# Splitting the float16 halves of key and query chunks in two pieces, in a fused agent-attention and mixture-of-experts kernel

## The chip, the cores and the metric

The kernel runs on one core of one Trainium2 chip. The metric is the device time of one execution in microseconds. TensorE (PE) multiplies matrices, VectorE (DVE) and ScalarE (ACT) do elementwise work, GpSimd (POOL) some more of it, and SyncE (SP) issues nearly all DMAs, in one queue and in order. Each engine works through its own list of instructions in order, and waits on semaphores for the others.

## The reference

There are four batches (B) of 11456 tokens (N) with 128 channels, 49 agents, eight experts with 1024 hidden units. All is float32.

```python
scale = 1.0 / np.sqrt(q.shape[-1])
def sm(a, b):
    s = scale * (a @ b.transpose(0, 2, 1))
    s = s - s.max(-1, keepdims=True)
    e = np.exp(s)
    return e / (e.sum(-1, keepdims=True) + 1e-09)
a2k = sm(agents, k)          # agents look at the keys
agent_v = a2k @ v
q2a = sm(q, agents)          # queries look at the agents
x = (q2a @ agent_v)          # then flattened to B*N tokens
...
expert_idx = np.argmax(x @ w_gate, axis=1)
gate_w = softmax(x @ w_gate)[expert_idx]      # written out in the original
h = np.maximum(xe @ w1[e], 0.0)
out[mask] = gate_w[mask, None] * (h @ w2[e])  # for the tokens of each expert
```

## The kernel before, in words

Tokens of a batch are cut into twelve chunks: eleven of 1024 tokens (a tile of 128 partitions by 8 by 128) and one of 192 (96 partitions by 2 by 128). For each batch the kernel first reads the keys (k) chunk by chunk, then the values (v), then the queries (q), and then sends all tokens of the batch through the one expert that most of them want; tokens of other experts are redone in blocks at the end.

The expert work is what everything else is woven around. It is cut into steps, 184 for a batch (23 groups of up to 512 tokens by 8 slices of the hidden layer), 736 in all. A step is: two matmuls of the first layer into a PSUM tile `ph` (L1535, L1536; four buffers), the ReLU of it on ACT into the high float16 half `hh[:, 0]` (L1538), the low half `hh[:, 1]` on DVE (L1539), and, five steps later, twelve matmuls of the second layer (L1553). Every eighth step DVE scales and empties the output tile (`yo`, L1566). While the steps of batch b run, the keys and values of batch b+1 and the last queries of batch b are prepared between them.

The order of that other work is written out by hand. Every piece of work is an event with a time counted in steps; `at(t, f)` puts it into a heap, `after(dt, f)` puts it dt steps behind the event that runs now. Events are traced in order of their times. Instructions of an event at time t may not stand ahead of the paced step's matmul at t - 1.5 on PE, of its ReLU at t - 2 on ACT, and of its low half at t - 2 on DVE. SP's instructions all stand in the order of their events.

A key or query chunk that is taken in the common way ("A") goes through these events; the lines are those of the profile:

- `use` and `load`: the chunk's load, issued from SP (L350) with up to three uses ahead, into one of eleven `ld` buffers;
- `squares` at t: ACT squares the tile and sums it by partition (L407, tile `jk`);
- `total` at t + 0.5: DVE makes a power-of-two scale of the sum in two tiny instructions, `hb` (L253) and `mul` (L257); POOL makes its inverse `div` (L260);
- `split` at t + 0.8 (batch 0: t + 1): ACT writes the high half of the scaled tile (`hi`, one instruction, L445), and DVE writes the low half (`lo`, one instruction, L449), which needs the high half; both are 128x1024;
- `turn_over` 4.5 steps later (batch 0: 2.5): SP issues a DMA transpose of both halves (L485) into `hT`, which has two buffers for keys and two for queries;
- `kscores` or `qscores` at t + 12 or so: 24 matmuls of `hT` with the agents (L550 to L552), whose results ACT (L579, keys) or DVE (L824, L828, queries) takes on.

Keys and queries of 1024 tokens that are split in this way from the first step on are 70 in number: queries 4 to 10 of batch 0, keys 3 to 10 and queries 0 to 10 of batch 1, keys and queries 0 to 10 of batches 2 and 3. Values go through the same `split` lines, but are not touched by the change. Two chunks (`PRE`: query 3 of batch 0 and key 2 of batch 1) are split before the first step.

Of the kernel before, what the change touches and what calls it, by code (L numbers as in the profile page):

```python
# [16 lines left out]
AF = mybir.ActivationFunctionType  # L17
ALU = mybir.AluOpType
# [32 lines left out]
QA, QB, QC, QB3, KL, LL, UD, RG, D1, DL = -27, 11, 13, 10.5, 12, 9.5, 2, 0.7, 0.5, 0  # L51
# [3 lines left out]
UDL = 1.5  # L55
LHH, LATER = 11, (1, 4, 6)
ES, SV0 = 2, 1.7
TFL = 104.2
VD3, UD0, QD9 = 1.3, 1.2, 1.5
TM2 = 1.7  # L60
QM0, QG0 = (-145.5, -141.85, -137.3), ("K", "V", "V")
KP = 2, 5
LO0, LQ3 = -135.5, -142.9
# [2 lines left out]
PRE = {(0, "q", 3): (-157, -147.5), (1, "k", 2): (-156.9, -145.4)}  # L66
TLQ = 5, 9.5, 14
GL = -141.6, -140.6
KS1 = [-140.6, -139.7] + [0.5 + 8.2 * i for i in range(10)]
KS2 = {0: 1.5, 1: 6.5}  # L70
# [6 lines left out]
DTR, DTQ, DTE, DEX, DST, DXS = 4.5, 2.5, 3, 6, 5, 0.5  # L77
# [18 lines left out]
def agent_moe_kernel(ctx, tc, q, k, v, agents, wg, w1, w2, out):  # L96
    nc = tc.nc
# [8 lines left out]
    chunks = [(c * CH, P, 8) for c in range(NCH)]  # L106
    if REM:
        chunks.append((NCH * CH, REM // 2, 2))
    NCK = len(chunks)
# [7 lines left out]
    scale = 1.0 / math.sqrt(D)  # L117
# [177 lines left out]
    def pick(x, c):  # L295
        return x[c % len(x)]
# [4 lines left out]
    now, count = [0], [0]  # L301

    def at(t, f, *a):
        count[0] += 1
        heapq.heappush(events, (t, count[0], f, a))

    def after(dt, f, *a):
        at(now[0] + dt, f, *a)

    def turns(gen, t, dt, n):  # L310
        for i in range(n):
            at(t + i * dt, next, gen, None)
# [3 lines left out]
    def attention(b):  # L316
        st = state[b]
        base = b * steps
        first, last = b == 0, b + 1 == B

        how = {}
# [110 lines left out]
        def split(src, c):  # L432
            with queued("D") if b < 2 else nullcontext():
                split1(src, c)

        def split1(src, c):
            _, p, t = chunks[c]
            x = loaded[b, src, c]
            hl = xpool.tile([P, 2, 8, D], F16, tag="hl", name="hl", bufs=HLB)
            hi, lo = hl[:, 0], hl[:, 1]  # L440
            m = SC[src, c][0][:p, :1]
            if pick(HI[b > 0][src], c) == "D" or (b, src, c) == (0, "q", 3):
                gate["HQ"] = nc.vector.tensor_scalar(hi[:p, :t, :], x[:p, :t, :], m, None, op0=ALU.mult)
            else:
                nc.scalar.activation(hi[:p, :t, :], x[:p, :t, :], AF.Copy, scale=m)  # L445
            if (b, src, c) in PRE:
                at(1.5 if b else LQ3, split_low, "WL" if b else "V", src, c, x, hl)
            elif pick(LO[b > 0][src], c) == "D":
                nc.vector.scalar_tensor_tensor(lo[:p, :t, :], x[:p, :t, :], m, hi[:p, :t, :], op0=ALU.mult, op1=ALU.subtract)  # L449
                split3(src, c, hl)  # L450
            else:
                after(0 if first else DXS, split2, src, c, x, hl)

        def split_low(behind, src, c, x, hl):
            _, p, t = chunks[c]
            with queued(behind):
                nc.vector.scalar_tensor_tensor(hl[:p, 1, :t, :], x[:p, :t, :], SC[src, c][0][:p, :1], hl[:p, 0, :t, :],
                                               op0=ALU.mult, op1=ALU.subtract)
            split3(src, c, hl)

        def split2(src, c, x, hl):
            _, p, t = chunks[c]
            m, xv = SC[src, c][0][:p, :1], x[:p, :t, :]
            if pick(XS[b > 0][src], c) == "D":
                nc.vector.tensor_scalar(xv, xv, m, None, op0=ALU.mult)
            else:
                nc.scalar.activation(xv, xv, AF.Copy, scale=m)
            nc.gpsimd.tensor_tensor(hl[:p, 1, :t, :], xv, hl[:p, 0, :t, :], op=ALU.subtract)
            split3(src, c, hl)

        def split3(src, c, hl):
            if src == "v":
                TT[src, c] = hl[:, 0], hl[:, 1]
                return
            if (b, src, c) in PRE:
                at(max(now[0], HT0[src]), turn_over, src, c, hl)
            else:
                after(0 if now[0] < 0 else DTQ if first else DTR, turn_over, src, c, hl)

        def turn_over(src, c, hl):  # L480
            _, p, t = chunks[c]
# [367 lines left out]
        def esplit1(c):  # L849
# [8 lines left out]
            if first and c == 2:  # L858
                at(TM2, eturn, c, m2)
            else:  # L860
# [181 lines left out]
        def use(t, src, c):  # L1042
            o = b, src, c
            uses.append((EARLY[o] if o in EARLY else PRE[o][0] if o in PRE else base + t, b, src, c))

        def prepare(t, src, c):
            if (b, src, c) in PRE:
                t = PRE[b, src, c][1] - base
            at(base + t, squares, src, c)
            at(base + t + (0 if first else D1), total, src, c)  # L1050
            at(base + t + (0.5 if first else UD + UDL if (src, c) == ("v", NCK - 1) else UD + UD0 if b > 1 and (src, c) == ("v", 0) else UD), total2, src, c)
            at(base + t + (UD + 1 + SV0 if (src, c) == ("v", 0) and not first else 1 if first else D1 + 0.3 if src != "v" else UD + UDL + 1 if c + 1 == NCK else UD + 1), transposed if how[src, c] in "CX" else split, src, c)

        ks, kt, kl, vt, vl = (KS0, KT0, KL0, VT0, VL0) if first else (KS, KT, KL, VT, VL)
        dl = 0 if first else DL
# [1 line left out]
        for x, f in ((AG0, agent_squares), (AG1, agent_sums), (AG2, agent_scale), (AG3, agent_split)):  # L1057
            at(base + ka - x, f)
        for c in range(NCK):
            t = KS1[c] - base if b == 1 and c < len(KS1) else ks + kt * c  # L1060
            use(t, "k", c)
            prepare(t, "k", c)
            s = KS2[c] - base if b == 1 and c in KS2 else t + kl
            at(base + s, kscores, c)
            at(base + s + dl, kmax, c)
        if b == 1:
            at(-137.35, kpiece, 0, KP[1], "P1")
        if first:
            at(LO0, load_on, 5)
        tk = t + kl + 2  # L1070
        for i in range(1 if first else 0, 3):
            at(base + tk + i, keymax, i)
        tv = tk + 4
        for c in range(NCK):
            t = tv + vt * c
# [25 lines left out]
        for c in range(NCK):  # L1101
            if first and c < NQ:
                t, ql_ = QS0[c], QL0[c]
            else:
                t = (Q0 + QC * (c - 3) if first and c > 2 else QA + QB * c if c < 3 else
                     QA + 2 * QB + (QB3 if last else QC) * (c - 2))
                ql_ = KLL if last and c > 2 else KL
                if not first and c < 2:
                    t, ql_ = (t - QE, ql_) if c == 0 else (t, ql_ + QL1)
            if 0 < b < B - 1 and c == 9:  # L1110
                ql_ += QD9
            use(-150 + 3 * c if first and 0 < c < NQ else t, "q", c)
            prepare(t, "q", c)
            at(base + t + ql_, qscores, c)
            t0, t3 = t + ql_ + DL, t + ql_ + 3
            if first and c < NQ:
                t0, t3 = -135.9 if c == 2 else QM0[c] + 0.1, (-145, -132.6, -132.5)[c]
            at(base + t0, qexp, c)
            tl = max(t + ql_ + (TL if first and c < NQ else LLL if last and c > 2 else LL), ta + (TLM if first else 4) + c / 2)
            if first and c < NQ:  # L1120
                tl = TLQ[c]
            end = min([x for x in starts if x > c] + [NCK]) - 1
            c0 = max(x for x in starts if x <= c)
            late_ = c0 * 16 + LAG + 8 - 6 * RG - 1 - LMG - LSP * (end - c)
            late_ = min(late_, (LT3 if last else LT) - 6 * RG - 1.5 - LSP * (NCK - 1 - c))
            tl = max(tl, min(tl + LX, late_))
            if c > 2 and tl >= t3 + ES + 6.5:
                t3 += ES
            at(base + t3, esplit, c)
            at(base + tl, logits, c)  # L1130
            if c + 1 in starts or c == NCK - 1:
                turns(route(c), base + tl + 1, RG, 6)
                tf = max(tl + 1 + 6 * RG, tw + 1)
                at(base + tf, factors, c)
                c0 = max(x for x in starts if x <= c)
                assert tf < c0 * 16 + LAG + 8, (b, c, tf)
# [477 lines left out]
    for b in range(B):  # L1614
        attention(b)
        steps_of.append(experts(b))
        turns(steps_of[b], b * steps, 1, steps + LAG + 2)
        turns(leftover_ranks(b), b * steps + (LT3 if b + 1 == B else LT), LTS3 if b + 1 == B else LTS, 6)

    for j in range(2 * E):  # L1620
        b, i = divmod(j, -(-2 * E // (B - 1)))
# [105 lines left out]
```

## Time and profile before

| | us |
|---|---|
| median of 3 runs (1076.25 to 1080.18) | 1076.61 |
| the profiled execution's own time | 1071.08 |
| its span, first to last instruction | 1069.3 |
| PE busy in the span | 1006.5 |
| DVE busy | 977.8 |
| ACT busy | 828.2 |

The profiled execution is one of its own, some 5 us quicker than the shown runs. The span is what the trace covers; 1.8 us of the execution lie around it. Busy times are those of the engine's instructions; a wait inside the program is the idle time ahead of an instruction, together with what ended it.

### The profile page before, as it was taken

Reading aid. Unit: us, or ns where it says so; the run is one execution under the profiler, and the core shown is the slowest. Engines: PE = TensorE matmul, PEld = TensorE weight load, DVE = VectorE, ACT = ScalarE, POOL = GpSimd, SP = SyncE. Lnnn points to the kernel's source line nnn. Section 1 sums busy time; section 2 is a strip of 40 time slices with the busy share of each in tenths; the row PEclk is TensorE's granted clock in tenths of the full one; section 3 lists DMA queues with packets and bytes.
Section 4 is the critical chain, followed back from the end, with each engine's and each line's share of the span. In section 5 each row is a group of like instructions: output and inputs, shape, how many; then the busy total and the mean of one; then the engine's idle time right before and its main releaser. Section 6 shows DMA issues by size and latency. Waiting matters only on the chain.

```text
span 1069.3 us, 35681 instructions
## 1 busy us (share of the span) xinstructions
PE 1006.5 (94%) x14586; PEld 816.8 (76%) x14586; DVE 977.8 (91%) x2256; ACT 828.2 (77%) x1519; POOL 251.5 (24%) x457
## 2 busy tenths in 40 slices
PE   7989999999999999999999999999999999999986
PEld 7878778777777877777777877777778778767885
DVE  5789999999999998999999998999999999899893
ACT  6668887888788878988788877988677667667674
POOL 1100001236100101334200001333200235171283
PEclk9999999999999999999999999999999999999999
DMA  9889998534699997544699997544556664434550
GB/s 322 273 228 216 203 215 188 140 96 150 166 233 227 222 190 198 159 148 163 160 242 220 225 190 201 154 160 144 144 132 145 159 142 102 148 116 147 170 194 16
DMA packets 265368, 188.39 MB, mean 176 GB/s; under 512 B 207129, under 2 KB 231282, under 8 KB 265200
## 3 DMA queue, kind: packets, MB, share of 16 engines
q1 hardware_dynamic: 263632, 183.82, 67.2%
q0 software_dynamic: 1568, 2.25, 1.1%
q8 instruction: 115, 1.88, 0.7%
q14 instruction: 53, 0.43, 0.1%
HBM read 99.75 MB, written 36.43 MB: 127 GB/s over the span
## 4 chain that ended last, share of the span: by engine, by line
DVE 43%; PE 28%; ACT 12%; issue 9%; DMA 3%; POOL 3%; SPq 0%; POOLq 0%; DVEq 0%; ACTq 0%
DVE hh L1539 16%; PE py L1553 13%; DVE hl L449 8%; PE ph L1535 5%; PE ph L1536 4%; ACT hh L1538 3%; ACT hl L445 3%; DVE yo L1566 3%; ACT jk L407 2%; DVE S L640 1%; DVE mq L824 1%; DVE mx L603 1%; DMA ld<-in_q_dram 1%; DVE E L828 1%; POOL out_dram L1437 1%
## 5 line engine op out<-in xcount | busy, mean ns | idle before, releaser
L1553 PEld LDWEIGHTS <-hh 128*128 128x128 f16 x8640 | 543.5, 98 | 165.5 <-issue 2.0
L1553 PE MATMUL py<-w2h,hh 128*128 128x128 f16 (+1 forms) x5760 | 601.8, 219 | 1.4 <-DVE Ld L878 0.9
L1553 PE MATMUL py<-w2l,hh 128*128 128x128 f16 (+1 forms) x2880 | 520.2, 219 | 0.0
L1539 DVE SCALAR_TENSOR_TENSOR hh<-ph,hh 128x512 f16<-128x512 f32 (+1 forms) x736 | 478.2, 668 | 21.8 <-ACT hh L1538 19.6
L1538 ACT ACTIVATE hh<-ph 128x512 f16<-128x512 f32 (+1 forms) x736 | 410.0, 581 | 96.5 <-PE ph L1536 90.2
L1535 PE MATMUL ph<-M,Ah 128*128 128x512 f16 (+1 forms) x736 | 274.0, 372 | 21.0 <-DVE hh L1539 20.4
L1536 PE MATMUL ph<-M,Al 128*128 128x512 f16 (+1 forms) x736 | 274.1, 373 | 0.0
L449 DVE SCALAR_TENSOR_TENSOR hl<-ld,mul,hl 128x1024 f16<-128x1024 f32 (+1 forms) x113 | 138.9, 1230 | 14.8 <-ACT hl L445 14.2
L445 ACT ACTIVATE hl<-ld,mul 128x1024 f16<-128x1024 f32 (+1 forms) x114 | 124.3, 1091 | 34.9 <-DVE mul L257 34.3
L407 ACT ACTIVATE jk<-ld 128x1024 f16<-128x1024 f32 (+1 forms) x122 | 122.2, 1001 | 6.1 <-DMA ld<-in_k_dram 4.1
L260 POOL TENSOR_SCALAR div<-hb,bits 128x1 int32<-128x1 int32 (+1 forms) x86 | 25.4, 295 | 378.6 <-DVE hb L253 372.7
L1536 PEld LDWEIGHTS <-Al 128*128 128x128 f16 x736 | 71.7, 97 | 28.9 <-issue 27.2
L1535 PEld LDWEIGHTS <-Ah 128*128 128x128 f16 x736 | 73.4, 100 | 2.0 <-issue 1.4
L1566 DVE TENSOR_TENSOR yo<-py,cs 128x512 f32<-128x512 f32 (+1 forms) x92 | 61.6, 670 | 0.9 <-PE py L1553 0.9
L657 POOL TENSOR_TENSOR es<-es,S 128x392 f32<-128x392 f32 (+1 forms) x33 | 32.2, 976 | 110.1 <-ACT S L645 99.1
L550 PE MATMUL ps_s<-agh,hT 128*128 128x49 f16 x572 | 51.8, 184 | 1.8 <-DMA hT<-hl 1.8
L551 PE MATMUL ps_s<-agl,hT 128*128 128x49 f16 x572 | 51.6, 184 | 0.0
L552 PE MATMUL ps_s<-agh,hT 128*128 128x49 f16 x572 | 51.6, 184 | 0.0
L550 PEld LDWEIGHTS <-hT 128*128 128x128 f16 (+1 forms) x590 | 47.9, 97 | 4.3 <-issue 2.1
L551 PEld LDWEIGHTS <-hT 128*128 128x128 f16 (+1 forms) x590 | 46.7, 96 | 0.6
L552 PEld LDWEIGHTS <-hT 128*128 128x128 f16 (+1 forms) x590 | 46.4, 96 | 0.0
L645 ACT ACTIVATE S<-S,ln 128x392 f32<-128x392 f32 (+1 forms) x48 | 27.6, 597 | 21.9 <-DVE S L640 21.7
(328 smaller groups left out, 1385.7 us busy)
## 6 DMA issues: line engine op xcount, KB each, us to landing
ld<-in_k_dram SPq DMA_DIRECT2D x44, 512.0 KB
ld<-in_v_dram SPq DMA_DIRECT2D x44, 512.0 KB
ld<-in_q_dram SPq DMA_DIRECT2D x44, 512.0 KB
out_dram<-yo SPq DMA_DIRECT2D x88, 256.0 KB
w2e<-in_moe_w_dram SPq DMA_DIRECT2D x18, 512.0 KB
w1e<-in_moe_w_dram SPq DMA_DIRECT2D x17, 512.0 KB
exps<-E SPq DMA_DIRECT2D x44, 196.0 KB
wn<-in_moe_w_dram SPq DMA_DIRECT2D x16, 512.0 KB
```

What stands on the lines that cost most here:

```text
L407: nc.scalar.activation(jk[:p, :t * D], x[:p, :t, :].rearrange("p t d -> p (t d)"), AF.Square, accum_out=ss[:p])
L445: nc.scalar.activation(hi[:p, :t, :], x[:p, :t, :], AF.Copy, scale=m)
L449: nc.vector.scalar_tensor_tensor(lo[:p, :t, :], x[:p, :t, :], m, hi[:p, :t, :], op0=ALU.mult, op1=ALU.subtract)
L550: nc.tensor.matmul(o, x[:, 0, i, :p], AG["h"], start=True, stop=False)
L551: nc.tensor.matmul(o, x[:, 0, i, :p], AG["l"], start=False, stop=False)
L552: nc.tensor.matmul(o, x[:, 1, i, :p], AG["h"], start=False, stop=True)
L1535: x1 = nc.tensor.matmul(ph[:, :nn], st['Ah'][:, f, :], m, start=True, stop=False)
L1536: nc.tensor.matmul(ph[:, :nn], st['Al'][:, f, :], m, start=False, stop=True)
L1538: x2 = nc.scalar.activation(hh[:, 0, :nn], ph[:, :nn], AF.Relu)
L1539: x3 = nc.vector.scalar_tensor_tensor(hh[:, 1, :nn], ph[:, :nn], 0.0, hh[:, 0, :nn], op0=ALU.max, op1=ALU.subtract)
L1553: mm_ = lambda l, r, **k: nc.tensor.matmul(o, l, r, skip_group_check=True, **k)
L1566: nc.vector.tensor_tensor(yo[:p, :n, :], py[:p, :n * D].rearrange("p (i d) -> p i d", d=D), cs.unsqueeze(2).broadcast_to([p, n, D]), op=AL ...
```

## The change

A key or query chunk of 1024 tokens that is split after time 0 is split in two pieces of 128x512 (four of the eight token slots each): `piece(0)` at the split's time, `piece(4)` two steps later (`HPC`), each with its own ACT and DVE instruction. The split's event comes one step later after the squares (`SPL`); `turn_over` follows the second piece by 2.5 steps (batch 0: 1.5) so that, counted from the squares, it comes one step later than before (batch 0: two). For the keys of batches 2 and 3 and for queries 0 to 8 (in batch 0: 5 to 8) the load, the squares, the scale and so the whole row come a step sooner (`KE`), and the scores stay where they were.

So for those chunks the squares move a step ahead, the first piece and the transpose stay at their old times, and the second piece comes two steps behind the first. For keys 3 to 10 of batch 1 and queries 9 and 10 the squares stay, the first piece comes one step later, the second three steps later, the transpose one step later (batch 0, queries 4, 9 and 10: two). Chunks of 192 tokens stay in one piece, a step later after their squares.

```diff
@@ -439,6 +442,15 @@  (split1)
             m = SC[src, c][0][:p, :1]
+            if now[0] > 0 and t == 8 and src != "v":
+                def piece(i):
+                    nc.scalar.activation(hi[:, i:i + 4], x[:, i:i + 4], AF.Copy, scale=m)
+                    nc.vector.scalar_tensor_tensor(lo[:, i:i + 4], x[:, i:i + 4], m, hi[:, i:i + 4], op0=ALU.mult, op1=ALU.subtract)
+                    if i:
+                        split3(src, c, hl)
+                piece(0)
+                after(HPC, piece, 4)
+                return
             if pick(HI[b > 0][src], c) == "D" or (b, src, c) == (0, "q", 3):
@@ -475,7 +487,7 @@  (split3)
-                after(0 if now[0] < 0 else DTQ if first else DTR, turn_over, src, c, hl)
+                after(0 if now[0] < 0 else DTQ - (SPL if (b, src, c) not in PRE else 0) if first else DTR - SPL - (HPL if chunks[c][2] == 8 else 0), turn_over, src, c, hl)
@@ -1049,7 +1061,7 @@  (prepare)
-            at(... 1 if first else D1 + 0.3 if src != "v" else ..., transposed if how[src, c] in "CX" else split, src, c)
+            at(... 1 + (SPL if base + t > 2 else 0) if first else D1 + 0.3 + SPL if src != "v" else ..., transposed if how[src, c] in "CX" else split, src, c)
@@ -1057,17 +1069,17 @@  (keys of a batch)
-            t = KS1[c] - base if b == 1 and c < len(KS1) else ks + kt * c
+            t = KS1[c] - base if b == 1 and c < len(KS1) else ks + kt * c - (KE if b > 1 else 0)
-            s = KS2[c] - base if b == 1 and c in KS2 else t + kl
+            s = KS2[c] - base if b == 1 and c in KS2 else t + kl + (KE if b > 1 else 0)
-        tk = t + kl + 2
+        tk = t + kl + 2 + (KE if b > 1 else 0)
@@ -1109,6 +1121,8 @@  (queries of a batch)
+            if not (first and c < 5) and c < 9:
+                t, ql_ = t - KE, ql_ + KE
```

with `SPL = 1`, `KE = 1`, `HPC, HPL = 2, 1`; before, `D1` is 0.5, `DTQ` 2.5 and `DTR` 4.5.

## Rows read from the trace of the kernel before

**Rows 1.** Windows: stretch, length; busy us of PE, PEld, DVE, ACT, POOL; clock.
```profile
67.00:184.00 117.00, 113.20 (x1685) 90.28 (x1684) 111.51 (x241) 94.56 (x168) 8.32 (x21) 1.00 0.97 219
...
264.00:424.00 160.00, 153.22 (x2287) 122.40 (x2285) 151.17 (x361) 129.19 (x230) 16.99 (x39) 1.00 0.89 205
...
508.00:664.00 156.00, 149.01 (x2216) 119.14 (x2214) 147.57 (x356) 127.06 (x228) 17.41 (x46) 1.00 0.95 210
...
750.00:910.00 160.00, 155.37 (x2161) 123.48 (x2161) 151.37 (x384) 113.60 (x215) 37.86 (x76) 1.00 0.60 138
```

**Rows 2.** Page, part 4: the chain that ended last, by engine.
```profile
DVE 43%; PE 28%; ACT 12%; issue 9%; DMA 3%; POOL 3%; SPq 0%; POOLq 0%; DVEq 0%; ACTq 0%
```

**Rows 3.** Waits of PE in the four stretches in order (total us, times, longest).
```profile
PE ph L1535 <- DVE hh L1539: 1.6, 4, 0.8
...
PE ph L1535 <- DVE hh L1539: 3.4, 6, 1.0
...
PE ph L1535 <- DVE hh L1539: 3.1, 6, 1.0
...
PE ph L1535 <- DVE hh L1539: 3.5, 8, 1.3
```

**Rows 4.** Waits of DVE for the high half, first and last of the four stretches.
```profile
DVE hl L449 <- ACT hl L445: 2.0, 4, 0.6
...
DVE hl L449 <- ACT hl L445: 1.0, 3, 0.6
```

**Rows 5.** Waits of ACT, whole span.
```profile
ACT hl L445 <- DVE mul L257: 34.3, 48, 1.9
```

**Rows 6.** Timeline of ACT, 389 to 395 us (start, us, line, what).
```profile
389.07 1.05 ACT L407 ACTIVATE jk<-ld 128x1024 f16<-128x1024 f32 x1
...
390.11 1.14 ACT L445 ACTIVATE hl<-ld,mul 128x1024 f16<-128x1024 f32 x1
391.15 1.07 ACT L1538 ACTIVATE hh<-ph 128x512 f16<-128x512 f32 x2
```

**Rows 7.** Timeline of DVE, the same stretch.
```profile
391.28 1.28 DVE L449 SCALAR_TENSOR_TENSOR hl<-ld,mul,hl 128x1024 f16<-128x1024 f32 x1
392.49 1.28 DVE L1539 SCALAR_TENSOR_TENSOR hh<-ph,hh 128x512 f16<-128x512 f32 x2
393.68 1.28 DVE L449 SCALAR_TENSOR_TENSOR hl<-ld,mul,hl 128x1024 f16<-128x1024 f32 x1
```

**Rows 8.** Timeline of PE: two steps without a wait, then the same stretch.
```profile
352.81 0.38 PE L1535 MATMUL ph<-M,Ah 128*128 128x512 f16 x1
...
353.91 0.38 PE L1535 MATMUL ph<-M,Ah 128*128 128x512 f16 x1
...
393.22 0.38 PE L1535 MATMUL ph<-M,Ah 128*128 128x512 f16 x1 [0.89 <-DVE hh L1539]
```

**Rows 9.** Timelines of DVE and ACT, 14 to 18 us: scaled halves of 128x512.
```profile
14.08 1.40 DVE L523 SCALAR_TENSOR_TENSOR xT<-pxT,mul,xT 128x512 f16<-128x512 f32 x2
15.40 0.35 DVE L595 COPY mx<-S 128x392 f32<-128x392 f32 x1
...
15.90 1.27 ACT L522 ACTIVATE xT<-pxT,mul 128x512 f16<-128x512 f32 x2 [0.40 <-DVE mul L257]
```

**Rows 10.** Timelines of DVE, SP, ACT and PE: key 3 of batch 3, a load.
```profile
562.01 1.29 DVE L449 SCALAR_TENSOR_TENSOR hl<-ld,mul,hl 128x1024 f16<-128x1024 f32 x1 [0.20 <-ACT hl L445]
...
557.30 0.42 SPq L350 DMA_DIRECT2D ld<-in_k_dram  x1
...
563.36 2.81 SPq L485 DMA_TRANSPOSE hT<-hl  x1
...
563.81 1.05 ACT L407 ACTIVATE jk<-ld 128x1024 f16<-128x1024 f32 x1
...
569.44 0.20 PE L550 MATMUL ps_s<-agh,hT 128*128 128x49 f16 x1
```

**Rows 11.** Waits of PE, 508 to 664 us: the one wait for a transpose.
```profile
PE ps_s L550 <- DMA hT<-hl: 1.8, 1, 1.8
```

More of the change, by code (lines that the diff above doesn't have):

```diff
@@ L60 @@
 TM2 = 1.7
+SPL = 1
+KE = 1
+HPC, HPL = 2, 1
 QM0, QG0 = (-145.5, -141.85, -137.3), ("K", "V", "V")
@@ L1051, in prepare @@
             at(base + t + (0.5 if first else UD + UDL if (src, c) == ("v", NCK - 1) else UD + UD0 if b > 1 and (src, c) == ("v", 0) else UD), total2, src, c)
-            at(base + t + (UD + 1 + SV0 if (src, c) == ("v", 0) and not first else 1 if first else D1 + 0.3 if src != "v" else UD + UDL + 1 if c + 1 == NCK else UD + 1), transposed if how[src, c] in "CX" else split, src, c)
+            at(base + t + (UD + 1 + SV0 if (src, c) == ("v", 0) and not first else 1 + (SPL if base + t > 2 else 0) if first else D1 + 0.3 + SPL if src != "v" else UD + UDL + 1 if c + 1 == NCK else UD + 1), transposed if how[src, c] in "CX" else split, src, c)
         ks, kt, kl, vt, vl = (KS0, KT0, KL0, VT0, VL0) if first else (KS, KT, KL, VT, VL)
```

## The prediction

> **What bounds the kernel now.** I read the windows view first, over the four stretches in which keys and queries are split and no values are [rows 1]. The reader is to see that two engines are full at once: of 593 us PE is busy for 570.8 and DVE for 561.6, so PE idles for 22.2 us and DVE for 31.4. ACT is busy for 464.4 and idles for 128.6. PE runs at full clock in all of them. Neither PE nor DVE can give much by itself; what can be got are the moments in which one waits for the other. The chain that ended last says the same of the whole span, with DVE ahead of PE and ACT third [rows 2].
>
> The waits say who holds whom. In these stretches PE stood 24 times, 11.6 us, in front of a step's first matmul until DVE had finished a low half and so freed a buffer of `ph` [rows 3]; that is half of PE's idle time there. DVE itself stood 20 times, 9.0 us over the four (from 2.0 in the first to 1.0 in the last), in front of a chunk's low half (L449) until ACT had written its high half (L445) [rows 4]. And ACT stood 48 times in the whole span, 34.3 us, in front of the high half until DVE had made the scale [rows 5].
>
> The timelines show how these hang together at one place. On ACT the squares (389.07) are followed by the high half (390.11) with no ReLU between them, so the step's next ReLU starts at 391.15, 2.08 us after the squares [rows 6]. DVE can start the low half at 391.28 only; the ReLU's low halves behind it start at 392.49 [rows 7]. PE, which needs the first of them, stood 0.89 us, until 393.22 [rows 8]. A step on PE that waits for nothing takes 353.91 - 352.81 = 1.10 us [rows 8], so one such pile-up eats most of what four `ph` buffers can bridge.
>
> **The change part by part.**
>
> *Two instructions for one, on DVE.* 70 chunks get a second low half. Two scaled halves of 128x512 took 15.40 - 14.08 = 1.32 us from start to start, 0.66 each [rows 9]; one of 128x1024 takes 392.49 - 391.28 = 1.21 [rows 7]. Instructions overlap their neighbours' ends, so starts are what counts: 1.32 - 1.21 = 0.11 us a chunk, 70 x 0.11 = 7.7 us more DVE work. Those of rows 9 read PSUM and ours read SBUF; the shape and the per-partition scale are the same, so I take their price. From below: an unscaled ReLU half of 128x512 takes (393.68 - 392.49) / 2 = 0.595 [rows 7], which makes two no dearer than one, 0. From above: by durations, 0.74 (1.40 less 0.66) twice against 1.28, 0.20 a chunk, 14 us. Nothing excludes any of these. Not all of it is paid in time: 7.7 us stand against 31.4 us of DVE's idle time in those stretches, but idle time at the wrong place doesn't help, and the chain runs mostly over DVE. I take +2 us, a quarter; the ends are 0 and the whole 14.
>
> *Two instructions for one, on ACT.* Two high halves of 128x512 took 1.27 us [rows 9], one of 128x1024 1.14 [rows 6]: 70 x 0.13 = 9.1 us. I cost them at nothing: ACT's 128.6 idle us hide them [rows 1]. Without that cover each would delay a ReLU by 0.13 us.
>
> *What the pieces take off the waits.* In the place of one 1.21 us block on DVE there are two of 0.66, two steps apart, so a ReLU's low half behind a piece comes 0.55 us sooner. The first high half takes ACT 1.27 / 2 = 0.64 instead of 1.14, about as long as DVE is busy with the ReLU half ahead of it (0.595), so DVE's wait for it, 9.0 / 20 = 0.45 us each [rows 4], should go. And with the squares a step further ahead, or the split a step later, a ReLU stands between squares and first piece and the scale is ready: ACT's wait for the scale, 34.3 / 48 = 0.71 us each [rows 5], should mostly go for keys and queries. These three are one chain, so I count only its end, PE's waits: 24 of 0.48 us each [rows 3]. A pile-up that loses 0.55 and often 0.45 more loses most such waits; but several of the 24 have no key or query split ahead of them. I take 9 of the 11.6 us. The ends are 0 (the waits move to other places) and 20: the 11.6, and DVE's 9.0 going to stretches where DVE is late without PE being seen to stand for it (11.6 + 9.0, rounded down).
>
> *The transpose.* SP's place for it is unchanged for most chunks, but in the place shown it already starts only 0.06 us after the low half ends (563.36 against 562.01 + 1.29) [rows 10], so it will start as much later as the second piece ends later: two steps, 2.2 us, and 0.66 - 1.21 = -0.55, together some 1.7 us; a step more for keys of batch 1. It was issued by 566.17 and its matmul came at 569.44, 3.27 us later [rows 10]; 1.6 us stay for its landing. In SP's timeline 18 of the 70 stand at most 4.3 us apart in this way. The stretch holds one wait for a transpose, 1.8 us, so landings are not far from mattering even now [rows 11]. What is queued on SP behind it (stores of `yo`, loads, the transpose of `mm`) waits as long. I take +1 us: one or two scores that stand for half a us or so. From below 0, from above 18 x 0.6 = 11 us (18 late by 0.6 each: half of the 1.7, less what has slack).
>
> *The moved loads.* Load and squares move together. A load whose issue ended at 557.72 has its squares at 563.81, 6.1 us later [rows 10]; if SP stands 1.7 us longer, 4.4 are left. I cost it at nothing, since ACT's waits in these stretches hold none for a load; without that slack it would be up to 1.7 us for a chunk. Ten small chunks and key 2 of batch 1 only have their split a step later: nothing.
>
> *A rule of the Trainium skill.* Rows 1 have DVE busy for 561.6 of 593 us, 95%, and ACT for 78%. The Trainium skill, Perfetto Trace Analysis, section Optimizing Scalar/DVE Operations, says that "grouping and performing larger operations can improve throughput if the engine is saturated", with about 60 ns of overhead for a DVE operation on SBUF, and that breaking up instructions may help where Scalar and Vector aren't saturated but cause bubbles elsewhere. For DVE it is the first sentence that applies, and it speaks against the change; for ACT the second. By its figure the added DVE work would be an estimated 4.2 us, and paid in full it would be a slower kernel unless the bubbles are worth more.
>
> *Sum.* -9 + 2 + 1 = -6 us. The profiled execution, 1071.1 us with a span of 1069.3, would come to 1065.1; it was quicker than the three runs shown, so on their median of 1076.6 I expect 1070.6.
>
> **The rivals.**
>
> *The waits only move.* Everything is at its place, but DVE is as full as before, and what PE gains at one step it stands for at a later one. For it: both engines at 95% or more [rows 1]. Against: PE's idle time is in few, short waits [rows 3]. Time: -2 to +2, 1076.
>
> *More falls than the waits counted.* DVE's own waits turn into time as well: -18 + 2 + 1 = -15, 1061.6. For it: DVE leads the chain [rows 2]. Against: PE was busy for 96% of these stretches [rows 1], so there are only 22.2 us to take.
>
> *The transpose comes late: slower.* Place: the first score matmul of a chunk (L550). Price: at 11 us instead of 1 the sum is -9 + 2 + 11 = +4, 1080.6. It decides where landing takes over 1.6 us after the issue ends. For it: the wait of 1.8 us [rows 11]. Against: it is a single one among 70.
>
> *DVE is the bound and the work is paid in full: slower.* This is the mechanism of the rule above, by the rows: at 14 us added, of which all counts, and 5 of the 9 us regained, 14 - 5 + 1 = +10, 1086.6. For it: DVE's 43% of the chain [rows 2]. Against: 31.4 us idle.
>
> **How the numbers follow.** Forecast 0.50, waits only move 0.17, more falls 0.15, transpose late 0.12, DVE paid in full 0.06. Half a per cent, 5.4 us, is about what a measurement of this kernel can tell from no change, so the forecast itself (-6, likely -2 to -11) lies close to that line: 0.28 of its 0.50 falls on the faster side, 0.22 on the same. With all of "more falls", faster is 0.43. Same: 0.22 + 0.15 + 0.02 of the late transpose = 0.39. Slower: the other 0.02, 0.10 and 0.06 = 0.18. The range reaches to 1061 (below it about half of "more falls") and to 1081 (above it half of "transpose late" and all of the last).
>
> **What would show it.** Right: 140 pieces of 128x512 at the lines of the high and the low half; DVE busy some 8 us up, ACT some 9; waits of L449 for L445 in these stretches near 2 us instead of 9; PE's waits for L1539 near 4 instead of 11.6. The prediction is wrong if PE shows new waits at L550 for `hT` of 3 us or more in sum, if the pieces take over 0.70 us from start to start, or if PE's waits for L1539 stay above 8 us.

## The result and the profile after

The changed kernel is slower: median 1087.51 us (1083.93 to 1092.03, six executions) against 1077.18 us of before (1076.25 to 1080.18, six), ratio 1.0093, 95% interval 1.0073 to 1.0112. Measured again it gave 1.0076 (1.0044 to 1.0108), and a third time 1.0049 (1.0023 to 1.0075), so 5 to 10 us are lost where 6 were forecast as gained.

The execution profiled after took 1091.71 us, span 1089.6, which is 20.3 more than the span of before. By PE's first step matmul (L1549 now, L1535 before) the first step starts 5.5 us later (72.53 against 67.07), the steps take 14.7 us more, and the rest 0.1. Some 7 of the 14.7 are not the change's: from step 46 to 138 of batch 3 PE stands in short waits with no releaser. Waits of this kind stand at the same steps in the trace of h1 below (5.9 us), whose batches 1 to 3 are before's. They are in just the six traces (after, e9, f1, g6, h1, h4) beside which before itself measured 1077 to 1079 us instead of 1071 to 1072.

The new names: L1549 and L1550 are the `ph` matmuls, L1553 the ReLU's low half, L447 and L448 the pieces (high, low), L457 and L461 what stays whole, L562 the first score matmul, L888 the logits, L890 their reduction.

Windows of the four stretches after, cut at the steps at which [rows 1] were cut:

```profile
72.50:193.60 121.10, 117.83 (x1710) 93.32 (x1710) 111.62 (x255) 96.06 (x180) 9.38 (x22) 0.96 0.83 192
274.10:436.50 162.40, 154.47 (x2285) 123.42 (x2283) 153.93 (x383) 132.74 (x253) 17.65 (x39) 0.99 0.87 202
520.50:676.60 156.10, 149.62 (x2222) 119.62 (x2222) 150.60 (x376) 130.75 (x248) 17.00 (x45) 1.00 0.90 210
762.00:928.60 166.60, 159.61 (x2173) 125.34 (x2173) 154.53 (x396) 115.58 (x227) 35.91 (x76) 0.99 0.58 135
```

The stretches are longer, and the clock is no longer 1.00 in all of them. Waits of PE in the four in order, each stretch behind "..." (total us, times, longest), beside [rows 3] and [rows 11]:

```profile
PE py L1567 <- DVE Ld L890: 1.9, 1, 1.9
...
PE ph L1549 <- DVE hh L1553: 0.2, 1, 0.2
...
PE ph L1549 <- DVE hh L1553: 2.3, 4, 0.8
PE ps_s L888 <- DMA M<-mm: 1.8, 1, 1.8
...
PE ps_s L562 <- DMA hT<-hl: 1.6, 2, 1.2
PE ph L1549 <- DVE hh L1553: 1.5, 5, 0.3
...
PE ph L1549 <- DVE hh L1553: 2.6, 6, 1.3
```

The waits that the change was counted on did fall, from 11.6 us to 6.6. In their place are single long ones: for the logits' reduction, for `M`, for `hT`. The page's groups of the pieces:

```profile
L447 ACT ACTIVATE hl<-ld,mul 128x512 f16<-128x512 f32 x140 | 97.9, 718 | 14.2 <-DVE mul L260 13.8
L448 DVE SCALAR_TENSOR_TENSOR hl<-ld,mul,hl 128x512 f16<-128x512 f32 x140 | 104.9, 753 | 1.6 <-ACT hl L447 1.2
```

There are 140 pieces. ACT's wait for the scale is 13.8 us instead of 34.3 [rows 5], DVE's for the high half 1.2 over the whole span. DVE is busy 985.1 us, 7.3 more than before; this total is a rough measure, since it is 13.2 us up in e3, which has the same pieces, and 6.3 in e4, which has none.

The prologue, on PE, after:

```profile
58.24 0.31 PE L765 MATMUL ps_small<-ident,av 128*128 128x128 f32 x1
59.92 1.12 PE L971 MATMUL pa<-w1e,av 128*128 128x512 f32 x2 [1.37 <-DMA w1e<-in_moe_w_dram]
60.88 0.71 PE L526 MATMUL pxT<-ident,ld 128*128 128x128 f32 x3
```

and before:

```profile
58.86 0.31 PE L753 MATMUL ps_small<-ident,av 128*128 128x128 f32 x1
59.01 1.04 PE L514 MATMUL pxT<-ident,ld 128*128 128x128 f32 x8
60.78 1.10 PE L959 MATMUL pa<-w1e,av 128*128 128x512 f32 x2 [0.74 <-ACT xF L520]
```

Before, eight transposes `pxT` fill the time until the expert's weights `w1e` have landed. After, `pa` comes first and PE stands 1.37 us for them, instead of 0.74 us for ACT. Windows of after with the granted clock (third number from the end):

```profile
61.00:78.00 17.00, 17.00 (x71) 13.38 (x70) 7.00 (x27) 7.60 (x15) 1.61 (x3) 0.50 0.96 298
132.70:136.10 3.40, 3.40 (x36) 2.40 (x32) 2.89 (x5) 1.19 (x2) 0.91 (x1) 0.50 1.49 217
392.10:395.50 3.40, 3.40 (x26) 2.64 (x24) 2.31 (x7) 1.36 (x3) 0.00 (x0) 0.50 0.92 178
774.40:777.80 3.40, 3.40 (x22) 2.45 (x21) 2.33 (x10) 0.65 (x2) 0.00 (x0) 0.50 0.12 22
```

The clock is at 0.50, 1.2 GHz, for 17 us right behind that stand, and for 3.4 us behind each of three others: for the reduction (PE resumed at 131.75), for `M` (391.57) and for `avs` (773.2). Before, no step ran at half clock.

### The profile page after: what moved, and what is told of

Same layout as the page of the kernel before. It is cut to its first block, busy times and chain, and to the rows that moved or that the text cites. A ratio compares the mean times of both kernels' runs of the same rounds, so it can differ in the third digit from the quotient of the medians.

```text
span 1089.6 us, 35840 instructions
## 1 busy us (share of the span) xinstructions
PE 1020.9 (94%) x14586; PEld 824.9 (76%) x14586; DVE 985.1 (90%) x2326; ACT 840.1 (77%) x1589; POOL 251.8 (23%) x457
## 4 chain that ended last, share of the span: by engine, by line
DVE 37%; PE 34%; ACT 11%; issue 7%; DMA 5%; POOL 4%; SPq 1%; another core or an unknown queue 0%; POOLq 0%; ACTq 0%; DVEq 0%
PE py L1567 15%; DVE hh L1553 15%; PE ph L1549 5%; PE ph L1550 5%; DVE hl L448 4%; ACT hh L1552 3%; ACT jk L410 3%; DVE hl L461 2%; DVE yo L1580 2%; DVE S L652 1%; ACT hl L457 1%; DVE mq L836 1%; DMA ld<-in_q_dram 1%; DMA out_dram<-yo 1%; ACT hl L447 1%
## 5 line engine op out<-in xcount | busy, mean ns | idle before, releaser
L1553 DVE SCALAR_TENSOR_TENSOR hh<-ph,hh 128x512 f16<-128x512 f32 (+1 forms) x736 | 479.0, 665 | 28.2 <-ACT hh L1552 24.9
L1549 PE MATMUL ph<-M,Ah 128*128 128x512 f16 (+1 forms) x736 | 276.5, 376 | 18.8 <-DVE hh L1553 17.5
L1550 PE MATMUL ph<-M,Al 128*128 128x512 f16 (+1 forms) x736 | 276.5, 376 | 0.5 <-issue 0.5
L263 POOL TENSOR_SCALAR div<-hb,bits 128x1 int32<-128x1 int32 (+1 forms) x86 | 28.3, 331 | 370.0 <-DVE hb L256 369.4
L447 ACT ACTIVATE hl<-ld,mul 128x512 f16<-128x512 f32 x140 | 97.9, 718 | 14.2 <-DVE mul L260 13.8
L448 DVE SCALAR_TENSOR_TENSOR hl<-ld,mul,hl 128x512 f16<-128x512 f32 x140 | 104.9, 753 | 1.6 <-ACT hl L447 1.2
L1550 PEld LDWEIGHTS <-Al 128*128 128x128 f16 x736 | 72.2, 98 | 27.8 <-issue 26.7
L1549 PEld LDWEIGHTS <-Ah 128*128 128x128 f16 x736 | 74.0, 101 | 3.1 <-issue 2.5
L562 PE MATMUL ps_s<-agh,hT 128*128 128x49 f16 x572 | 52.1, 184 | 2.5 <-DMA hT<-hl 1.6
L457 ACT ACTIVATE hl<-ld,mul 128x1024 f16<-128x1024 f32 (+1 forms) x44 | 43.7, 1000 | 12.9 <-DVE mul L260 12.6
L461 DVE SCALAR_TENSOR_TENSOR hl<-ld,mul,hl 128x1024 f16<-128x1024 f32 (+1 forms) x43 | 48.9, 1139 | 4.5 <-ACT hl L457 3.7
L562 PEld LDWEIGHTS <-hT 128*128 128x128 f16 (+1 forms) x590 | 48.0, 97 | 3.8 <-DMA hT<-hl 2.0
L563 PEld LDWEIGHTS <-hT 128*128 128x128 f16 (+1 forms) x590 | 46.8, 97 | 1.7 <-issue 1.4
```

What stands on the lines that cost most here:

```text
L447: nc.scalar.activation(hi[:, i:i + 4], x[:, i:i + 4], AF.Copy, scale=m)
L448: nc.vector.scalar_tensor_tensor(lo[:, i:i + 4], x[:, i:i + 4], m, hi[:, i:i + 4], op0=ALU.mult, op1=ALU.subtract)
L562: nc.tensor.matmul(o, x[:, 0, i, :p], AG["h"], start=True, stop=False)
L563: nc.tensor.matmul(o, x[:, 0, i, :p], AG["l"], start=False, stop=False)
L1549: x1 = nc.tensor.matmul(ph[:, :nn], st['Ah'][:, f, :], m, start=True, stop=False)
L1550: nc.tensor.matmul(ph[:, :nn], st['Al'][:, f, :], m, start=False, stop=True)
```

## The experiments

My theory at the start was A with B, with C as the rival; the others came up on the way. **A**: the prologue's new order costs. **B**: late transposes cost (rival of the prediction). **C**: the added DVE work is paid (the other rival); **C0**: only in batch 0. **D**: the later splits cost by themselves. **The waits only move**: even with nothing late there is no gain.

**e1: two keys' transposes back.** Keys 0 and 1 of batch 1 are not split but transposed on TensorE, and the line that moves the splits moves them too.

```diff
-D1 + 0.3 + SPL if src != "v"
+D1 + 0.3 + SPL * (b != 1 or src != "k" or c > 1) if src != "v"
```

> The changed kernel, with one thing undone: the transposes on TensorE of keys 0 and 1 of batch 1, which the diff moved a step later together with the splits, are back in their old place, so that eight of them stand again between the small sum and the product pa in the prologue. Theory A (the prologue: PE reaches pa sooner, stands 1.4 us for w1e, falls to half clock at 61 us and runs 17 us so): the first step starts at 67 us again instead of 72.5, and the time falls by 5.5 to 8 us, to a ratio to before of 1.002 to 1.004. Rival B (the steps alone make the loss, the prologue's delay is taken up by what follows): the time stays at 1.007 to 1.011.

Measured: 1.0041 (1.0025 to 1.0058). The first step starts at 66.83, and the window from 60.6 to 78 has clock 1.00. A holds for this part; about half of the loss is left, measured against the changed kernel's 1.0093 and 1.0076 (against its third measurement, 1.0049, most of it). Waits of PE in the four stretches of e1:

```profile
PE ph L1549 <- DVE hh L1553: 1.4, 3, 0.8
...
PE ps_s L562 <- DMA hT<-hl: 0.6, 1, 0.6
...
PE ph L1549 <- DVE hh L1553: 2.0, 4, 0.8
PE ps_s L888 <- DMA M<-mm: 1.8, 1, 1.8
PE ps_s L562 <- DMA hT<-hl: 1.4, 3, 1.0
...
PE ps_s L562 <- DMA hT<-hl: 2.2, 3, 1.4
PE ps_s L888 <- DMA M<-mm: 1.9, 1, 1.9
...
PE ph L1549 <- DVE hh L1553: 1.0, 3, 0.3
...
PE ph L1549 <- DVE hh L1553: 2.4, 5, 1.2
```

Here the waits for the low half are 6.8 us, 4.8 less than before; those for `hT` and, behind them in SP's queue, for `M` are 7.9 us where before had 1.8. How far such sums move from one execution to another is seen in e2, whose order in these stretches is before's: 9.2 and 2.9. The other four traces with this order (after, e8, e9, f1) have 5.5 to 6.6 and 3.8 to 6.5, so the fall and the rise are there in all five, and the fall goes 2 to 4 us beyond e2's.

**e2: only that, in the kernel before.**

```diff
-D1 + 0.3 if src != "v"
+D1 + 0.3 + ((b, src) == (1, "k") and c < 2) if src != "v"
```

> The kernel before, with one thing done: the transposes on TensorE of keys 0 and 1 of batch 1 a step later, as in the changed kernel; no pieces, no other move. Theory A: PE stands for w1e in the prologue, the clock falls there, the first step starts some 5 us later, and the time rises by 5 to 8 us, ratio 1.005 to 1.0075. Rival B: within 0.2% of before.

Measured: 1.0030 (1.0005 to 1.0055), below A's range, with an interval that reaches into B's. In the profiled execution PE stands 1.34 us for `w1e`, the clock is at half from 60.6 to 64.0, and the first step starts at 68.97, 1.9 us late. The twelve executions lie in two groups: nine from 1070.5 to 1076.0 us at mean clocks of 0.991 to 0.997, three from 1080.0 to 1083.0 at 0.980 to 0.988. A's mechanism is in the trace; its size is open.

**e3: only the cut, in place** (`SPL = 0`, `KE = 0`, `HPC, HPL = 0, 0`).

> The kernel before with the key and query splits in two pieces, one right behind the other in the old place: no step between them, no split or load moved, transposes in their old place. Theory C (the 7.3 us more on DVE are paid in full, as DVE leads the chain): ratio 1.006 to 1.008. Rival B (the loss comes from transposes that start later behind the second piece): the second piece ends only 0.1 us later than the whole did, so within 0.2% of before, at most +2 us.

Measured: 1.0044 (1.0027 to 1.0061), with PE's waits for `hT` and `M` at 1.0 us over the span. So there is a loss with no transpose late. It lies below C's range and above B's; C looked right, at a smaller price.

**e4: whole, but late.** The whole split is put off by `HPC` in place of the pieces; the two keys are back as in e1.

```diff
+if not late and now[0] > 0 and chunks[c][2] == 8 and src != "v":
+    after(HPC, split1, src, c, True)
+    return
```

> The changed kernel with the two keys of e1 back in their old place, and with each key or query split whole again, at the time of the second piece; loads and transposes as in the changed kernel. No DVE work is added. Theory B (late transposes): PE stands for hT at the score matmuls and, behind the queue of transposes, for M at the logits, 4 us or more in sum, and the time is above before by 4 to 8 us, 1.004 to 1.0075. Rival C (the added DVE work): within 0.2% of before or faster.

Measured: 1.0082 (1.0053 to 1.0111). The size is above B's, but the mechanism is B's only in part: PE's waits for transposes add up to 3.0 us over the span, and those for the ReLU's low half rose from before's 20.4 to 24.7. So it doesn't tell a late transpose from a whole block at another place.

**e5, e6, e7: the distance.** All are e1 with, in turn, `HPC, HPL = 0, -1`; the same with whole halves; and `HPC, HPL = 1, 0`.

> As e1 (the changed kernel, keys 0 and 1 of batch 1 transposed in their old place), with the second piece right behind the first instead of two steps later; loads, splits and SP's place for the transposes as in the changed kernel. Theory B (late transposes): the second piece ends two steps, 2.2 us, sooner, PE's waits for transposes fall from e1's 9.6 us to 3 or less, and the ratio from 1.004 to 0.998 to 1.000. Rival C (added DVE work, as e3 showed 1.0044 for it): it stays at 1.003 to 1.005.

> As e5 with the split whole, in one instruction on each engine: only the loads a step sooner and the splits a step later are left of the change, and SP's place for the transposes. Theory C: no DVE work is added, so it is faster than e5 by 3 to 5 us; with the gain that the prediction put on the squares lying further ahead, 0.995 to 0.999. Theory B alone: like e5, within 0.2%. Rival D (the splits a step later cost something by themselves): above 1.002.

> As e1 with the second piece one step after the first instead of two. Theory B: PE's waits for transposes lie between those of e1 (9.6 us) and of e5, about 5, and the ratio is 1.000 to 1.003. Rival C: as e1, 1.004, whatever the distance.

Measured: 1.0041 (1.0023 to 1.0059), 1.0054 (1.0035 to 1.0074), 1.0054 (1.0037 to 1.0072). None is told from e1. In e5 PE waits 0.7 us for transposes in the four stretches instead of e1's 7.9, as B expected, but the time stayed: B falls as the cause of the loss. (The expectations' 9.6 us is more than the 8.0 that e1's trace shows for `hT` and `M` over the whole span.) The waits for the low half went back from 6.8 to 10.8:

```profile
PE ph L1549 <- DVE hh L1553: 1.7, 4, 0.8
...
PE ph L1549 <- DVE hh L1553: 3.6, 5, 1.7
...
PE ph L1549 <- DVE hh L1553: 2.2, 5, 0.5
...
PE ph L1549 <- DVE hh L1553: 3.3, 8, 0.8
```

So the distance between the pieces goes with fewer of those waits and with later transposes: at no step between them, e3 and e5 have 9.8 and 10.8 us of the first, e7 with one step 7.9, the kernels with two 5.5 to 6.8. In time the two about cancel. e6 has no added DVE work and is no faster, which speaks against C as well; it lies in D's range, though its trace has another wait, told at g6.

**e8, e9: the changed kernel again.**

> The changed kernel once more, on the chip of e5 to e7. Theory A: beside e1's 1.0041 it has the prologue's 2 us that e2's trace showed (first step at 69.0 instead of 67.1) or, where the clock stays at half for 17 us, about 8; ratio 1.006 to 1.010. The stalls of batch 3 (6.9 us from its step 46 to 138 in the first profile, with no releaser in the trace) are not in e1, whose order there is the same: if they belong to the kernel they come again, if they were of that one execution they don't.

> The changed kernel once more, on the chip of f1, for the comparison. As in e8 there should be two groups of times, some 4 us above before and some 11 us above it, the upper one at lower clocks; ratio 1.006 to 1.010 by how many fall into which. Theory A1: the upper group is there and f1 has none of it. Rival A2: both kernels have the same groups.

Measured: 1.0076 (1.0044 to 1.0108) and 1.0049 (1.0023 to 1.0075). e8 has two groups, five executions from 1074.3 to 1075.6 at clocks of 0.991 to 0.995 and six from 1082.1 to 1087.7 at 0.981 to 0.992; e9 isn't in two groups and lies below its expected range; it spreads from 1079.6 to 1094.1, its two longest at 0.983 and 0.981. e8's lower group is 3.2 us above its before (1074.67 against 1071.44), no more than e1's 4.4, so what sets e8 apart from e1 is its upper group. The waits without a releaser in batch 3 came again in e9, beside a before of 1078.1 us, and not in e8, beside one of 1071.4: they aren't the kernel's.

The windows behind the stand for `w1e` in e2, e8 and e9 (stands of 1.34, 1.72 and 1.19 us), with the clock third from the end:

```profile
60.60:64.00 3.40, 3.40 (x14) 2.47 (x13) 1.44 (x6) 0.00 (x0) 0.00 (x0) 0.51 0.91 316
...
60.60:67.40 6.80, 6.80 (x31) 5.75 (x29) 1.66 (x7) 1.76 (x3) 0.90 (x1) 0.50 1.11 281
...
61.00:84.80 23.80, 23.80 (x115) 19.25 (x113) 13.00 (x37) 10.36 (x20) 2.02 (x3) 0.50 0.92 234
```

In all four traces in which `pa` stands in this way (these and after) the clock is at half from 60.6 or 61.0 on, for 3.4 to 23.8 us. In the thirteen traces with the two keys' transposes in their old place it is 1.00 from 58 to 66 us. The first step is late by about half of the time at half clock that lies ahead of it: 1.9 us for 3.4, 3.3 (70.39) for 6.8, 5.5 for 11.5 and 6.0 (73.10) for 12.1. So the traces show no delay in the prologue besides the half clock.

**g1: batch 0 as before.** `L` is `(b > 1 or (b == 1 and src == "q"))`; pieces, later splits and their shorter delays hold only where `L`, and queries are loaded sooner only for b > 0.

> The changed kernel with the whole change (pieces, splits a step later, queries' loads a step sooner) kept out of batch 0, whose order is that of before, prologue included; from batch 1 on as changed. Theory C0 (in batch 0 the added DVE work is paid, +2.9 us in e1's trace, and from batch 1 on gain and late transposes nearly cancel): some 3 us less than e1, ratio 1.000 to 1.002. Rival (the loss is spread over all batches): as e1, 1.003 to 1.005.

Measured: 1.0010 (0.9995 to 1.0026). C0's place holds: batch 0 is worth e1's 1.0041 less 1.0010, 3.3 us (the two intervals just touch). Whether it is the added work that is paid there this doesn't tell.

**h1, h4: the two halves of batch 0.** h1 is e3 with pieces only for batch 0's queries and batch 1's keys. h4 has no pieces, `SPL` only for keys of batch 1 from number 2 on, `KE` only for queries 5 to 8 of batch 0.

> As e3 (splits in two pieces, one right behind the other in the old place, nothing moved), but only for the chunks split during batch 0 (its queries and the keys of batch 1); batches 1 to 3 as before. Theory C0 (the added DVE work is paid in batch 0): most of e3's 1.0044, that is 1.0025 to 1.004, with PE at step 45 standing over 2 us for DVE's reduction of the logits instead of 1.1. Rival (the added work is paid wherever pieces are): about a third of e3's, 1.001 to 1.002.

> The complement in batch 0: splits whole, but a step later for the keys of batch 1 from number 2 on, and the last queries of batch 0 loaded a step sooner with their split at the old place, as in the changed kernel; no pieces, and batches 1 to 3 as before. Theory C0 (in batch 0 the pieces cost, not the moves): within 0.15% of before. Rival D (the later split costs): 1.002 or more.

Measured: h1 1.0044 (1.0024 to 1.0063), h4 1.0024 (1.0004 to 1.0044). h1 cuts 15 chunks and costs what e3's 70 cost, so C falls: 15 x 0.12 is only 1.8 us of DVE work, and the other 55 cuts, 6.6 us of it, cost nothing that the two ratios (each good to some 2 us) can tell. h4 lies above C0's expectation and in D's, with an interval that reaches down to 1.0004: the moves cost something in batch 0 as well. What the pieces of h1 do is seen at step 45 on DVE:

```profile
125.10 0.68 DVE L1553 SCALAR_TENSOR_TENSOR hh<-ph,hh 128x512 f16<-128x512 f32 x1
125.70 1.74 DVE L448 SCALAR_TENSOR_TENSOR hl<-ld,mul,hl 128x512 f16<-128x512 f32 x2
127.36 0.29 DVE L890 TENSOR_REDUCE Ld<-ps_y 128x72 f32<-128x144 f32 x1
```

and on PE:

```profile
127.71 0.26 PE L1567 MATMUL py<-w2h,hh 128*128 128x128 f16 x1 [2.37 <-DVE Ld L890]
```

The same place before, on DVE and on PE:

```profile
124.48 0.68 DVE L1539 SCALAR_TENSOR_TENSOR hh<-ph,hh 128x512 f16<-128x512 f32 x1
125.08 0.30 DVE L878 TENSOR_REDUCE Ld<-ps_y 128x72 f32<-128x144 f32 x1
125.78 1.28 DVE L449 SCALAR_TENSOR_TENSOR hl<-ld,mul,hl 128x1024 f16<-128x1024 f32 x1 [0.40 <-ACT hl L445]
```

```profile
125.43 0.22 PE L1553 MATMUL py<-w2h,hh 128*128 128x128 f16 x1 [0.93 <-DVE Ld L878]
```

Before, the low half stands behind the reduction that frees a PSUM buffer for `py`. Cut, its pieces stand ahead of it, and PE waits 2.37 us instead of 0.93. Why they come ahead of it there the traces don't show. In h1 the clock then is at half from 127.6 to 131.0. A second such place follows: the logits (L888) wait 1.8 us instead of 0.7 for `yo`, and the clock is at half from 165.2 to 168.6. e3's trace has both stands (2.4 and 1.8 us) with no half clock behind them, and its first 184 steps take 3.9 us more than before's, so the half clock isn't needed for the loss. In the changed kernel the first is the wait of 1.9 us shown above; the second is 0.9 us there. These stands and the half clock behind them are what the trace shows of the 4.7 us; the rest isn't assigned.

**g2, g6, g7: nothing late.** g2 is g1 with `KE = 3` and `HPC, HPL = 2, -1`; g6 has `KE = 2` and `HPC, HPL = 1, -1`; g7 is g6 with keys 0 to 3 of batches 2 and 3 whole and in their old places.

> As g1, with keys and queries loaded and squared three steps sooner instead of one, so that the first piece comes two steps before the place in g1 and the second ends about when the whole low half ended before; SP's place for the transposes as before. Theory B (from batch 1 on only the late transposes eat the gain): PE's waits for transposes fall to 2 us or less, the shorter waits for the ReLU's low half stay, and it is faster than before by 2 to 5 us, ratio 0.995 to 0.998. Rival (the waits only move): within 0.2% of g1.

> As g2 (batch 0 as before, pieces from batch 1 on, the second on time), with the pieces one step apart and the loads two steps sooner instead of three. If the gain of the pieces is there to be had once nothing comes late: 0.995 to 0.998. If the waits only move, as g2 showed: 0.999 to 1.002.

> As g6, with keys 0 to 3 of batches 2 and 3 (those split around the turn of a batch) whole and at their old places too, so that no squares wait there for a load that stands on SP behind two transposes (g6: 5.6 us on ACT, 4.2 us on PE, half clock for 6.8 us after it). If that was what ate the gain in g6: 0.996 to 0.999. If there is no gain to be had from pieces: 0.999 to 1.002, as g6.

Measured: 1.0016 (0.9997 to 1.0035), 1.0004 (0.9983 to 1.0026), 1.0002 (0.9988 to 1.0017). g6's trace has one late load at the turn of a batch. SP's timeline there, and the waits from 311 to 320 us:

```profile
298.82 9.57 SPq L497 DMA_TRANSPOSE hT<-hl  x2
308.44 0.57 SPq L353 DMA_DIRECT2D ld<-in_k_dram  x1
```

```profile
ACT jk L410 <- DMA ld<-in_k_dram: 5.6, 1, 5.6
...
PE py L1567 <- ACT hh L1552: 4.2, 1, 4.2
```

The key's load stands behind two transposes on SP, the squares that now come sooner wait for it, and the ReLU queued behind them too; e6 has the same at the same place (6.2 us on ACT, 3.8 on PE). g7 takes this out and still ends at before. Its waits for the low half in the four stretches, with none for a transpose, are 13.5 us:

```profile
PE ph L1549 <- DVE hh L1553: 1.6, 4, 0.8
...
PE ph L1549 <- DVE hh L1553: 5.3, 7, 2.8
...
PE ph L1549 <- DVE hh L1553: 2.6, 9, 0.4
...
PE ph L1549 <- DVE hh L1553: 4.0, 8, 1.2
```

In g2, with the pieces two steps apart, the waits for the low half stay lower, 8.5 us, and those for transposes are at 2.1 us, as before:

```profile
PE ph L1549 <- DVE hh L1553: 1.4, 3, 0.8
...
PE ph L1549 <- DVE hh L1553: 2.7, 3, 1.7
...
PE ph L1549 <- DVE hh L1553: 0.6, 3, 0.2
...
PE ph L1549 <- DVE hh L1553: 3.8, 8, 0.9
```

Yet these stretches take 595.7 us where the same steps before take 594.6: a new wait of 1.7 us for DVE stands at L732, and the clock is at half for 3.4 us behind it. So with the transposes on time there is no gain that these runs can tell, whether the counted waits come back (g7) or others take their place (g2). That the added DVE work, 5.6 to 6.6 us for the 47 to 55 chunks cut here, eats a gain of the same size isn't excluded. No version beat before.

**f1: the stand filled.** Twelve transposes of the identity go in front of `pa` in the prologue.

```diff
+if first and j == 0:
+    for i in range(12):
+        nc.tensor.transpose(pa[:, i % 4 * P:(i % 4 + 1) * P], ident, ident)
```

> The changed kernel with twelve transposes of the identity on TensorE put in front of the product pa in the prologue (into pa's own PSUM tile, written over by pa), so that PE has work while it waits for w1e; they add work and nothing is taken away. Theory A1 (what costs in the prologue is PE's stand in front of pa, after which the clock falls in some executions): the executions of e8 above 1080 us go, and the median comes to that of e1, ratio 1.003 to 1.005. Rival A2 (the late transposes of the two keys cost by being late, clock or not): as e8, 1.006 to 1.009, or more by the added 1 to 2 us.

Measured: 1.0043 (1.0026 to 1.0060), beside e9's 1.0049 on the same chip. Nine of ten executions lie from 1081.0 to 1086.1 us; one took 1092.67, and its trace has the clock at half from 54.0 to 67.7 us. The median is in A1's range, but so is e9's own, and in the one trace the clock fell before `pa`'s place (59 us), so f1 doesn't tell the two theories apart. The four traces at e8 tie the half clock to the stand; that the stand alone brings it down is not shown.

## Why the prediction was wrong

None of the three signs that were to show it wrong is in the profile after: no 3 us of new waits for `hT` (1.6 us, as against 1.8), pieces at 0.66 us, PE's waits for the low half at 6.6 us. The signs of being right came nearly all, and the time went the other way: it was lost at places that the signs didn't cover, and the waits that did fall weren't time.

**The edit that was missed.** "Ten small chunks and key 2 of batch 1 only have their split a step later: nothing" left out that the same line schedules the transposes of keys 0 and 1 of batch 1, in the prologue. They covered PE's wait for `w1e`. This costs 3.2 us by e2, and 0.35%, 3.8 us, between e8 and e1 (whose intervals overlap), but only 0.9 us between e9 and e1. In every trace that shows it, it is half clock behind PE's stand, 3.4 to 23.8 us long.

**"I take +2 us, a quarter" for the DVE work.** The work was sized right: a piece takes 0.66 us from start to start in e3, a whole half 1.20, which is 0.12 a cut and 8.4 us for 70 where 7.7 were worked out. But its price isn't a share of the work. As far as the traces show it, it lies in the order: pieces stand ahead of a reduction and of a `yo` that PE waits for, in batch 0. That is 4.7 us alone (h1), 3.3 in the changed kernel (e1 less g1, the moves of h4 included); h1 and h4 together would be 7.3, so the two don't add up, and why is open. The rule cited from the Trainium skill (Perfetto Trace Analysis, section Optimizing Scalar/DVE Operations) spoke against the change and had the sign. The trace doesn't agree with overhead as the reason: its estimate was 4.2 us of added work, 8.4 were measured, and a fifth of the cuts cost as much as all.

**"I take 9 of the 11.6 us."** The mechanism was there: ACT's wait for the scale, DVE's for the high half and PE's for the low half all fell. The last fell by 4.8 to 5.0 us, about half. And no run shows it as a gain in time: where the transposes came late they added more than it (e1), where the pieces stood together or nothing was late it came back (e5, g7), and where it stayed in part other waits came (g2). Of the rivals, "the waits only move" fits this term best. 11.6 us was also one execution's sum: e2's, in the same order, is 9.2.

**"I take +1 us" for the transposes.** PE's waits behind them rose by 6.1 us in e1, 2.4 for `hT` and 3.7 for `M`, and by 2.0 to 4.7 in after, e8, e9 and f1: inside the bounds of 0 and 11, and two to six times the size taken. `M` was named as queued behind them but not priced. Taking these waits away alone gave nothing (e5), since the others came back.

**Moved loads at nothing** held for the kernel as changed; at two steps, or with whole halves, one load cost about 4 us on PE (g6, e6).

Together: 3.8 (prologue), 3.3 (batch 0) and 1.1 (batches 1 to 3, g1, whose interval includes 0) make 8.2 us, e8's 0.76%. They must, since they are e8 less e1, e1 less g1, and g1; the sum is a way to read the three runs and adds no evidence. Why the changed kernel measured 0.93%, 0.76% and 0.49% in turn is not settled beyond the chance that the half clock brings in.

## What to carry to other kernels

Read a changed scheduling line for everything that it dispatches, in the prologue too: here the transposes of two keys, which the change's words don't name, may cost as much as all the rest. Where two engines are both full, a wait that is read from the profile is not time to be had; count it only if what the freed engine does next is also named. A cut instruction is priced by what it stands ahead of, more than by its added length.

## What was not expected of the hardware

Single stands of PE of 1.2 to 2.0 us are followed by the granted clock at 0.50 in some executions and not in others; only behind the stand for `w1e` was it so in all four traces. In the changed kernel's profile four stands were so followed: 17 us at half clock after the prologue's, 3.4 us after each of three others. In e1 the stands for the reduction (2.0 us), for `M` (1.9) and for `avs` (1.7) are the same, and no step ran at half clock. Nor does it take so long a stand. In g1 the clock is at half for 10.2 us from 73.8 on, behind waits of 0.77, 0.48 and 0.41 us that before has alike, at full clock:

```profile
73.80:84.00 10.20, 10.20 (x62) 8.25 (x61) 6.58 (x15) 3.81 (x7) 0.00 (x0) 0.50 1.15 268
```

A step matmul takes 0.63 us at 0.50 and 0.38 at 1.00. So one stand costs its length or, by chance, several times that; e8's two groups lie some 8 us apart.
